# Cosine attention with a two-layer MLP: batch 1's norms moved into batch 0's visits, batch 0's row sums inverted on ScalarE, batch 2 turned by DMA

## The chip, the cores and the metric

The kernel runs on one core of a Trainium2 chip. The metric is the device time of one execution in microseconds. A core has TensorE (PE in the profile, its weight loads PEld), VectorE (DVE), ScalarE (ACT), GpSimd (POOL) and SyncE (SP), each with a queue of its own that it works off in order, and 16 DMA engines. Matmul results land in PSUM; everything else lies in SBUF.

## The reference

Eight batches, 12 heads, 448 positions, 64 elements per head. Attention on normalised queries and keys, then two matrix products with a leaky ReLU between them:

```python
q_n = q / (np.linalg.norm(q, axis=-1, keepdims=True) + 1e-06)
k_n = k / (np.linalg.norm(k, axis=-1, keepdims=True) + 1e-06)
scores = np.matmul(q_n, k_n.transpose(0, 1, 3, 2)) / tau          # tau = 0.1
scores = scores - np.max(scores, axis=-1, keepdims=True)
attn = np.exp(scores)
attn = attn / (np.sum(attn, axis=-1, keepdims=True) + 1e-09)
attn_out = np.matmul(attn, v)
x = attn_out.transpose(0, 2, 1, 3).reshape(B * S, H * D)          # 3584 x 768
h = x @ w_in                                                      # 768 x 2048
out = np.maximum(0.01 * h, h) @ w_out                             # 2048 x 768
```

The scores are bounded because q and k have unit length, so the kernel leaves the maximum out.

## The kernel before, in words

Every instruction is put on its engine in the order in which the program is written (a manual schedule): an engine that waits holds back all that stands behind it in its queue. Inputs are cast to bf16 by the loads, which GpSimd's queue issues.

**A batch's steps.** The 448 positions are held as 112 partitions times 4. The 12 heads are 6 pairs (p) and 3 groups (g) of four heads; group g holds pairs 2g and 2g+1. A batch's q and k are normalised by `norm_squares` (x times x), `norm_reduce` (sum over 64 elements, on VectorE), `norm_root` (Ln and Exp with factor 0.5, on ScalarE), `norm_inverse` (add 1e-6, reciprocal, on VectorE) and `norm_apply` (multiply, two instructions for each group, on the engine given; `V` is VectorE, `P` GpSimd, `A` ScalarE). `norm_sums` is squares on VectorE and the reduce. Then the normalised q and k are turned, so that the head's elements lie on partitions: either by `turn_pair` (eight transposing matmuls for a pair into one PSUM tile of the pool `pmm`, then two copies) or by `turn`, one DMA transpose for a whole batch on SP's queue. Batches 0 to 2 take `turn_pair`, batches 3 to 7 `turn`.

`scores` computes half a pair's scores (two PSUM tiles of the pool `psc`, which has two) and their exponentials on ScalarE (L234). For a group, `weigh` is called twice, with s = 0 and 1. At s = 0 it makes the row sums on TensorE (`sums`, a PSUM tile `sm` of the pool `ppv`, which has two), inverts them (`inverse`, L262, a reciprocal on VectorE) and multiplies the first half of the values (`values`, the other `ppv` tile); `x_write` on VectorE scales the result into x. At s = 1 `values` needs a `ppv` tile again, the one that the reciprocal has read.

**Dense work.** x is cut into pieces; piece 0 is columns 0 to 255 of batch 0, piece 1 the next 128, then one piece for each batch. For a piece, `layer1` is 16 groups of 6 matmuls (L306), each followed by a leaky ReLU on ScalarE (L311), and `layer2` is 2 groups of 16 matmuls for every 128 tokens (L319), each followed by a copy on ScalarE (L325) and an output DMA on SP's queue. Both use the pool `pmm`, which has two tiles.

**Order.** An opening stretch written out by hand works through the first 256 columns of batch 0 (`part_scores` instead of `scores`), with the loads of batch 0, both weight matrices and batch 1 (in thirds, one for each group, then v). Then comes the loop over batches b and visits n = 0 to 11, a visit being half a pair. In a visit stand, in this order: the scores (batch 0: the remaining 192 columns, from visit 2 on), one owed `weigh` (a group's two are owed after its last visit, so they fall into the two visits that follow: 4 and 5, 8 and 9, and 0 and 1 of the next batch), the norm steps for later batches and the loads (`second_part` for batch 0, `after_scores` for the others), dense work until a budget is spent (`fill(budget(b, n))`, in planned microseconds), and the `turn_pair` calls that the table `turns` names. Where layer 1 is due and no `weigh` is owed, half a microsecond of it is put between a visit's two exponentials. The budgets run evenly from 0 to the end of piece 1 over the first 27 visits (32.22 planned us); the plan counts 0.67 for a layer-1 group of piece 0, 0.35 for one of piece 1 and 2.65 for a layer-2 group.

**Buffers that the steps touch.** The pool `bfpool` has four q and k tiles, so batch 2's loads take batch 0's; `vpool` has two, so batch 2's v waits for the last `values` of batch 0; `inp` holds one q_n and one k_n, so a batch's squares wait until the batch before is turned.

**Where the norms of batches 1 and 2 stand.** Before the change, the squares of batch 1's first group are at visit 2 of batch 0 on GpSimd, its apply at visit 7 and its turns at visits 9 and 10; the other two groups are normalised in visits 0 to 3 of batch 1 and turned at visits 3 to 5. Batch 2's `norm_sums` are at visits 6 and 7 of batch 1, its apply at 8 and 9, its six `turn_pair` at visits 10, 11 and visit 1 of batch 2.

Of the kernel before, what the change touches and what calls it, by code (L numbers as in the profile page):

```python
# [16 lines left out]
def kernel(  # L17
# [18 lines left out]
    nc = tc.nc  # L36
# [47 lines left out]
    def load(b, what, g0=0, g1=G):  # L84
        src = {"q": q_r, "k": k_r, "v": v_r}[what]
        if (what, b) not in st:
            if what == "v":
                st[what, b] = vpool.tile([PK, H, NT, D], BF16, name="v_bf")
            else:
                st[what, b] = bfpool.tile([PK, H, NT, D], BF16, name="qk_bf")  # L90
        if g1 - g0 == G:
            nc.gpsimd.dma_start(out=st[what, b], in_=src[b])  # L92
            return
        for g in range(g0, g1):
            nc.gpsimd.dma_start(out=st[what, b][:, g::G], in_=src[b][:, g::G])
# [19 lines left out]
    def norm_squares(b, what, eng, g0=0, g1=G):  # L115
        if (what + "n", b) not in st:
            st[what + "n", b] = inp.tile([PK, G, 2, NT, 2, D], BF16, name=f"{what}_n")
            st[what + "i", b] = small.tile([PK, G, 4, NT], F32, name=f"{what}_ni")
        for g in range(g0, g1):
            x, sq = by_quad(st[what, b])[:, g], squares(b, what, g, g + 1)[:, 0]  # L120
            if eng is nc.scalar:
                nc.scalar.activation(sq, x, func=ACTF.Square)
            else:
                eng.tensor_mul(sq, x, x)  # L124

    def norm_reduce(b, what, g0=0, g1=G):
        nc.vector.tensor_reduce(  # L127
            st[what + "i", b][:, g0:g1].rearrange("p g a t -> p (g a) t"),
            squares(b, what, g0, g1).rearrange("p g a t d -> p (g a) t d"),
            axis=AX.X, op=ALU.add,  # L130
        )
# [5 lines left out]
    def norm_root(b, what, g0=0, g1=G):  # L137
        ni = st[what + "i", b][:, g0:g1]
        nc.scalar.activation(ni, ni, func=ACTF.Ln, bias=tiny[:PK])
        nc.scalar.activation(ni, ni, func=ACTF.Exp, scale=0.5)  # L140

    def norm_inverse(b, what, g0=0, g1=G):
        ni = st[what + "i", b][:, g0:g1]
        nc.vector.tensor_scalar_add(ni, ni, 1e-6)
        nc.vector.reciprocal(ni, ni)  # L145

    def norm_apply(b, what, eng, g0=0, g1=G):
        x, xn, ni = by_quad(st[what, b]), st[what + "n", b], st[what + "i", b]
        for g in range(g0, g1):
            for j in range(2):  # L150
                ni_j = ni[:, g, 2 * j : 2 * j + 2]
                eng.tensor_tensor(  # L152
                    out=xn[:, g, j].rearrange("p t h d -> p h t d"),
                    in0=x[:, g, 2 * j : 2 * j + 2],
                    in1=ni_j.unsqueeze(3).to_broadcast([PK, 2, NT, D]),
                    op=ALU.mult,
                )
# [36 lines left out]
    def scores(b, p, half, hold=False):  # L194

        qT, kT = st["qT", b], st["kT", b]
        if half == 0:
            st["pe", b, p] = epool.tile([PK, NT, 2, S], BF16, name="pe")
        wide = 128 if b > 2 else PK
        for i in range(2):  # L200
            ki = 2 * half + i
            sc = psc.tile([128, 2, 512], F32, name="sc")
            o = p * S + ki * PK
            for a in range(2):
                r = slice(64 * a, 64 * a + 64)
                nc.tensor.matmul(  # L206
                    out=sc[:wide, a, :S], lhsT=kT[r, o : o + wide],
                    rhs=qT[r, p * S : (p + 1) * S], start=True, stop=True,
                )
            st["exp", i] = (st["pe", b, p][:, ki], sc[:PK, :, :S])  # L210
            if i == 0 or not hold:
                exponential(i)
# [46 lines left out]

    def inverse(b, g, sm, c0=0, c1=S):  # L260
        st["rs", b, g] = wk.tile([128, S], F32, name="rs")
        nc.vector.reciprocal(st["rs", b, g][:, c0:c1], sm[:, c0:c1])  # L262
        if ("x", b) not in st:
            x_place(b)

# [184 lines left out]
        at[0] += 1  # L450


    def second_part(n):
        if n == 2:
            norm_squares(1, "q", P, 0, 1)
            norm_squares(1, "k", P, 0, 1)
        elif n == 4:
            norm_reduce(1, "q", 0, 1)
            norm_reduce(1, "k", 0, 1)
        elif n == 6:  # L460
            norm_root(1, "q", 0, 1)
            norm_root(1, "k", 0, 1)
        elif n == 7:
            norm_inverse(1, "q", 0, 1)
            norm_inverse(1, "k", 0, 1)
            norm_apply(1, "q", V, 0, 1)
            norm_apply(1, "k", P, 0, 1)


    def after_scores(b, n):  # L470
        if b + 2 < B and b > 1 and n < 2:
            load(b + 2, "qk"[n])
        if b + 1 == B:
            return
        if b > 1 and n == 2:
            load(b + 1, "v")
        if b == 1:
            if n == 0:
                load(2, "q")
                norm_sums(1, "q", 1, 2)  # L480
                norm_sums(1, "k", 1, 2)
            elif n == 1:
                load(2, "k")
                norm_root(1, "q", 1, 2)
                norm_root(1, "k", 1, 2)
                norm_sums(1, "q", 2, 3)
                norm_sums(1, "k", 2, 3)
            elif n == 2:
                load(2, "v")
                for what in "qk":  # L490
                    norm_inverse(1, what, 1, 2)
                    norm_apply(1, what, P, 1, 2)
                norm_root(1, "q", 2, 3)
                norm_root(1, "k", 2, 3)
            elif n == 3:
                for what in "qk":
                    norm_inverse(1, what, 2, 3)
                    norm_apply(1, what, P, 2, 3)
            elif n == 5:
                load(3, "q")  # L500
            elif n == 6:
                norm_sums(2, "q")
                load(3, "k")
            elif n == 7:
                norm_sums(2, "k")
            elif n == 8:
                norm_root(2, "q")
                norm_inverse(2, "q")
                norm_apply(2, "q", P)
            elif n == 9:  # L510
                norm_root(2, "k")
                norm_inverse(2, "k")
                norm_apply(2, "k", V, 0, 1)
                norm_apply(2, "k", P, 1, 3)
        elif n == 2:
            norm_sums(b + 1, "q")
        elif n == 3:
            norm_sums(b + 1, "k")
        elif n == 4:
            norm_root(b + 1, "q")  # L520
        elif n == 5:
            norm_root(b + 1, "k")
            norm_inverse(b + 1, "q")
            norm_apply(b + 1, "q", P)
        elif n == 6:
            norm_inverse(b + 1, "k")
            norm_apply(b + 1, "k", P)
        elif n == 7:
            turn(b + 1, "q")
        elif n == 9:  # L530
            turn(b + 1, "k")

    turns = {
        (0, 9): (1, 0), (0, 10): (1, 1), (1, 3): (1, 2), (1, 4): (1, 3), (1, 5): (1, 4, 5), (1, 10): (2, 0, 1),
        (1, 11): (2, 2, 3), (2, 1): (2, 4, 5),
    }

    def after_dense(b, n):
# [6 lines left out]
    def budget(b, n):  # L545
        i = 12 * b + n + 1
        if i <= 27:
            return piece_end[1] * i / 27
        c, i = divmod(i - 3, 12)
        c = c - 1  # L550
        return piece_end[c] + (piece_end[c + 1] - piece_end[c]) * i / 12

    owed = []
    for b in range(B):
        for p in range(HP):
            for half in range(2):
                n = 2 * p + half
                hold = b > 0 and not owed and dense[at[0]][1] < 2.0
                if b > 0:
                    scores(b, p, half, hold)  # L560
                elif p > 0:
                    part_scores(p, half, *two)
                if owed:
                    weigh(*owed.pop(0))
                if half == 1 and p % 2 == 1:
                    c = two if b == 0 else ()
                    owed += [(b, p // 2, 0, *c), (b, p // 2, 1, *c)]
                if hold:
                    fill(spent[0] + 0.5)
                    exponential(1)  # L570
                if b == 0:
                    second_part(n)
                else:
                    after_scores(b, n)
                fill(budget(b, n))
                after_dense(b, n)
    fill(spent[0] + 1.0)
# [39 lines left out]
```

## Time and profile before

| | |
|---|---|
| median of 11 runs | 478.92 us (476.91 to 482.03) |
| the profiled execution | 480.06 us |
| its span, first to last instruction | 477.6 us |
| mean granted TensorE clock | 0.986 |
| busy: PE, DVE, ACT, POOL | 436.6, 219.1, 269.8, 126.6 us |
| chain that ended last: PE, DVE, ACT, DMA | 79%, 11%, 4%, 3% of the span |

The span covers the instructions; the execution has 2.5 us around it. A group row of the profile gives line, engine, operation, the tiles written and read with their shapes, the count, the busy time and the mean, and at its end the idle time of the engine ahead of these instructions and what released it. These rows name the operations of the change:

```profile
L262 DVE RECIPROCAL rs<-pv 128x448 f32<-128x448 f32 x21 | 62.0, 2954 | 144.2 <-PE pv L239 144.2
L262 DVE RECIPROCAL rs<-pv 128x256 f32<-128x256 f32 x3 | 5.3, 1753 | 3.2 <-PE pv L239 3.2
L262 DVE RECIPROCAL rs<-pv 128x192 f32<-128x192 f32 x3 | 4.1, 1357 | 10.1 <-PE pv L239 10.0
L188 DVE COPY qT<-mm 128x448 bf16<-128x448 bf16 x18 | 6.9, 386 | 5.4 <-PE mm L180 5.0
```

The columns 256 and 192 belong to batch 0; the idle time ahead of a reciprocal is VectorE waiting for row sums, which costs nothing by itself. In the timeline, batch 0's visits run from about 39 to 61 us, batch 1's from 61.4 to 108.7, batch 2's from 108.7 to 160.

### The profile page before, as it was taken

How to read it: one execution, taken by the hardware profiler on the slowest of the kernel's cores; microseconds unless marked ns; L12 is line 12 of the kernel's file. 1: busy time of each engine (PE TensorE's matmuls, PEld its weight loads, DVE VectorE, ACT ScalarE, POOL GpSimd, SP SyncE). 2: the span in 40 equal slices, each digit the busy share in tenths (PEclk: the TensorE clock that was granted, in tenths of full speed). 3: DMA queues.
4: the chain of work that ended last, by engine and by line, in shares of the span. 5: the costliest groups of instructions: out<-in, count | busy, mean ns of one | idle time of the engine just before them, and what ended most of it. 6: DMA issues, size and time to landing. Idle time of an engine off the chain costs nothing.

```text
span 477.6 us, 8541 instructions
## 1 busy us (share of the span) xinstructions
PE 436.6 (91%) x3632; PEld 222.4 (47%) x3632; DVE 219.1 (46%) x269; ACT 269.8 (56%) x445; POOL 126.6 (27%) x150
## 2 busy tenths in 40 slices
PE   0788978779899999989899999998999999999996
PEld 0456634454344554444334554444434554454463
DVE  5964677967913186206823186318711311321000
ACT  3766665836764557654674557664765567533411
POOL 7652308064083013800083013700180000000000
PEclk9999998979999999998999999999999999999999
DMA  9999991808529660493329560355034210020022
GB/s 115 207 201 203 194 175 28 113 2 126 81 52 138 126 109 1 71 212 56 53 50 135 130 108 1 59 125 92 0 59 92 60 41 1 18 66 18 0 67 66
DMA packets 73924, 41.23 MB, mean 86 GB/s; under 512 B 29600, under 2 KB 73120, under 8 KB 73888
## 3 DMA queue, kind: packets, MB, share of 16 engines
q0 software_dynamic: 37728, 22.81, 34.6%
q1 hardware_dynamic: 36160, 17.90, 16.0%
q8 instruction: 28, 0.46, 0.4%
q14 instruction: 8, 0.07, 0.0%
HBM read 45.61 MB, written 11.01 MB: 119 GB/s over the span
## 4 chain that ended last, share of the span: by engine, by line
PE 79%; DVE 11%; ACT 4%; DMA 3%; issue 2%; SPq 0%; POOL 0%; POOLq 0%; ACTq 0%; DVEq 0%
PE mm L319 29%; PE mm L306 28%; PE pv L239 12%; PE sc L206 7%; DVE rs L262 3%; DVE k_ni L127 2%; DMA kT<-k_n 2%; ACT pe L234 2%; PE sc L224 1%; DVE k_n L124 1%; DVE q_n L124 1%; PE mm L180 1%; DVE q_ni L127 1%; DMA qk_bf<-in_q_dram 1%; ACT hT L311 1%
## 5 line engine op out<-in xcount | busy, mean ns | idle before, releaser
L234 ACT ACTIVATE pe<-sc 112x896 bf16<-112x896 f32 (+2 forms) x192 | 168.1, 917 | 14.1 <-PE sc L224 7.9
L306 PE MATMUL mm<-xT,w_in_sb 128*128 128x512 bf16 (+3 forms) x864 | 157.4, 335 | 1.1 <-ACT hT L311 0.9
L319 PE MATMUL mm<-w_out_sb,hT 128*128 128x384 bf16 x896 | 155.3, 329 | 0.0
L262 DVE RECIPROCAL rs<-pv 128x448 f32<-128x448 f32 (+2 forms) x27 | 71.4, 2643 | 157.6 <-PE pv L239 157.5
L319 PEld LDWEIGHTS <-hT 128*128 128x128 bf16 x896 | 85.3, 98 | 67.6 <-issue 14.6
L306 PEld LDWEIGHTS <-w_in_sb 128*128 128x128 bf16 x864 | 77.8, 99 | 76.5 <-issue 17.1
L311 ACT ACTIVATE hT<-mm 128x512 bf16<-128x512 f32 (+3 forms) x144 | 71.9, 502 | 69.4 <-PE mm L306 69.0
L325 ACT COPY osb<-mm 128x384 f32<-128x384 f32 x56 | 26.8, 478 | 105.7 <-PE mm L319 70.8
L152 POOL TENSOR_TENSOR q_n<-qk_bf,q_ni 112x512 bf16<-112x512 bf16 x40 | 41.3, 1061 | 103.5 <-DVE q_ni L145 64.4
L206 PE MATMUL sc<-qT,kT 64*128 64x448 bf16 (+1 forms) x336 | 50.1, 362 | 10.4 <-ACT pe L234 7.2
L239 PE MATMUL pv<-pe,v_bf 112*32 112x448 bf16 (+2 forms) x864 | 48.8, 349 | 9.7 <-DVE rs L262 9.7
L152 POOL TENSOR_TENSOR k_n<-qk_bf,k_ni 112x512 bf16<-112x512 bf16 x44 | 46.6, 1085 | 15.4 <-DVE k_ni L145 15.4
L239 PEld LDWEIGHTS <-v_bf 112*32 112x32 bf16 x864 | 21.6, 100 | 30.0 <-issue 19.5
L92 POOL DMA_DIRECT2D v_bf<-in_v_dram x8 | 7.6, 944 | 101.8 <-PE pv L239 101.2
L206 PEld LDWEIGHTS <-kT 64*128 64x128 bf16 (+1 forms) x336 | 13.2, 103 | 40.4 <-issue 36.0
L127 DVE TENSOR_REDUCE q_ni<-q_n 112x16 f32<-112x1024 bf16 (+1 forms) x12 | 27.4, 2284 | 0.3
L127 DVE TENSOR_REDUCE k_ni<-k_n 112x16 f32<-112x1024 bf16 (+1 forms) x12 | 27.4, 2283 | 0.3
L239 PE MATMUL pv<-pe,ones 112*32 112x448 bf16 (+2 forms) x432 | 25.1, 350 | 1.0 <-ACT pe L234 1.0
L281 DVE TENSOR_TENSOR xT<-pv,rs 128x384 bf16<-128x384 f32 (+2 forms) x30 | 14.3, 477 | 22.9 <-PE pv L239 21.4
L278 DVE TENSOR_TENSOR xT<-pv,rs 128x448 bf16<-128x448 f32 x24 | 15.0, 624 | 19.4 <-PE pv L239 18.1
L180 PE MATMUL mm<-ident,q_n 112*128 112x112 bf16 x72 | 7.8, 243 | 10.7 <-DVE q_n L152 10.5
L124 DVE TENSOR_TENSOR q_n<-qk_bf 112x1024 bf16<-112x1024 bf16 x21 | 14.1, 718 | 4.6 <-DMA qk_bf<-in_q_dram 4.6
(42 smaller groups left out, 154.8 us busy)
## 6 DMA issues: line engine op xcount, KB each, us to landing
v_bf<-in_v_dram POOLq DMA_DIRECT2D x8, 672.0 KB, 7.9
qk_bf<-in_q_dram POOLq DMA_DIRECT2D x6, 672.0 KB, 7.5
qk_bf<-in_k_dram POOLq DMA_DIRECT2D x6, 672.0 KB, 10.7
w_in_sb<-in_moe_w_in_dram POOLq DMA_DIRECT2D x4, 768.0 KB, 19.8
w_out_sb<-in_moe_w_out_dram POOLq DMA_DIRECT2D x2, 1536.0 KB, 28.6
out_dram<-osb SPq DMA_DIRECT2D x16, 168.0 KB, 2.6
out_dram<-osb SPq DMA_DIRECT2D x16, 144.0 KB, 2.1
out_dram<-osb SPq DMA_DIRECT2D x16, 120.0 KB, 2.0
```

The lines of the kernel that those rows point to most:

```text
L124: eng.tensor_mul(sq, x, x)
L127: nc.vector.tensor_reduce(st[what + "i", b][:, g0:g1].rearrange("p g a t -> p (g a) t"), squares(b, what, g0, g1).rearrange("p g a t d -> ...
L152: eng.tensor_tensor(out=xn[:, g, j].rearrange("p t h d -> p h t d"), in0=x[:, g, 2 * j : 2 * j + 2], in1=ni_j.unsqueeze(3).to_broadcast([P ...
L206: nc.tensor.matmul(out=sc[:wide, a, :S], lhsT=kT[r, o : o + wide], rhs=qT[r, p * S : (p + 1) * S], start=True, stop=True,)
L234: nc.scalar.activation(out=pe, in_=sc, func=ACTF.Exp, scale=inv_tau)
L239: nc.tensor.matmul(out=dst[32 * a : 32 * a + 32, c0:c1], lhsT=weights(a, ki), rhs=st["pe", b, 2 * g + a // 2][:, ki, a % 2, c0:c1], start= ...
L262: nc.vector.reciprocal(st["rs", b, g][:, c0:c1], sm[:, c0:c1])
L278: nc.vector.tensor_mul(x[:, kt, 64:512], po, rs)
L306: nc.tensor.matmul(out=pm[:, :n], lhsT=w_in_sb[:, kt, m * 128 : (m + 1) * 128], rhs=st["x", b][:, kt, x0 : x0 + n], start=(kt == 0), stop= ...
L311: nc.scalar.activation(out=st["h", c][:, m, :n], in_=pm[:, :n], func=ACTF.Prelu, alpha=0.01)
L319: nc.tensor.matmul(out=po[:, :NH], lhsT=st["h", c][:, m, j0 : j0 + 128], rhs=w_out_sb[:, m, n * NH : (n + 1) * NH], start=(m == 0), stop=( ...
L325: nc.scalar.copy(out=osb, in_=po[:, :NH])
```

## The change

`inverse` for batch 0 is an Ln and an Exp with factor -1 on ScalarE instead of the reciprocal. `second_part` and batch 1's list in `after_scores` are replaced by `early`, which moves batch 1's norm steps to visits 0 to 11 of batch 0 and visits 0 and 1 of batch 1, with all three groups' squares on GpSimd, q applied on VectorE and k on GpSimd. Its turns move to visits 7, 8, 10 and 11 of batch 0 and visit 2 of batch 1. Batch 2's norms move from visits 6 to 9 of batch 1 to visits 3 to 7, its k is applied on VectorE throughout, and it is turned by two DMA transposes at visit 9 of batch 1 in place of the six `turn_pair`. The loads of batch 2's q and k move to visits 8 and 9 of batch 0, its v to visit 0 of batch 1, batch 3's q and k to visits 1 and 2. Scores of batch 2 take 128 keys' columns (its turned tiles are padded) instead of 112. Budgets are 1 planned us a visit in batch 0 and then even to the end of piece 1.

```diff
-        wide = 128 if b > 2 else PK
+        wide = 128 if b > 1 else PK
...
     def inverse(b, g, sm, c0=0, c1=S):
         st["rs", b, g] = wk.tile([128, S], F32, name="rs")
-        nc.vector.reciprocal(st["rs", b, g][:, c0:c1], sm[:, c0:c1])
+        rs = st["rs", b, g][:, c0:c1]
+        if b == 0:
+            nc.scalar.activation(rs, sm[:, c0:c1], func=ACTF.Ln)
+            nc.scalar.activation(rs, rs, func=ACTF.Exp, scale=-1.0)
+        else:
+            nc.vector.reciprocal(rs, sm[:, c0:c1])
...
-    def second_part(n):
...
+    def step(b, what, g0, g1, *steps):
+
+        for name, eng in steps:
+            if name == "squares":
+                norm_squares(b, what, eng, g0, g1)
+            elif name == "reduce":
+                norm_reduce(b, what, g0, g1)
+            elif name == "root":
+                norm_root(b, what, g0, g1)
+            else:
+                norm_inverse(b, what, g0, g1)
+                norm_apply(b, what, eng, g0, g1)
+
+    def early(b, n):
+        def both(to, g0, g1, name, eq=None, ek=None):
+            step(to, "q", g0, g1, (name, eq))
+            step(to, "k", g0, g1, (name, ek))
+
+        if b == 0:
+            if n == 0:
+                both(1, 0, 1, "squares", P, P)
+            elif n == 2:
+                both(1, 0, 1, "reduce")
+            elif n == 3:
+                both(1, 1, 2, "squares", P, P)
+            elif n == 4:
+                both(1, 0, 1, "root")
+            elif n == 5:
+                both(1, 0, 1, "apply", V, P)
+            elif n == 6:
+                both(1, 1, 2, "reduce")
+            elif n == 8:
+                both(1, 1, 2, "root")
+                both(1, 2, 3, "squares", P, P)
+                load(2, "q")
+            elif n == 9:
+                both(1, 1, 2, "apply", V, P)
+                load(2, "k")
+            elif n == 11:
+                both(1, 2, 3, "reduce")
+        elif n == 0:
+            both(1, 2, 3, "root")
+            load(2, "v")
+        elif n == 1:
+            both(1, 2, 3, "apply", V, P)
+            load(3, "q")
+        elif n == 2:
+            load(3, "k")
+        elif n == 3:
+            norm_sums(2, "q")
+        elif n == 5:
+            norm_sums(2, "k")
         elif n == 6:
-            norm_root(1, "q", 0, 1)
-            norm_root(1, "k", 0, 1)
+            step(2, "q", 0, 3, ("root", A), ("apply", P))
         elif n == 7:
...
+            step(2, "k", 0, 3, ("root", A), ("apply", V))
+        elif n == 9:
+            turn(2, "k")
+            turn(2, "q")
 
     def after_scores(b, n):
-        if b + 2 < B and b > 1 and n < 2:
+        if b < 2:
+            return early(b, n)
+        if b + 2 < B and n < 2:
             load(b + 2, "qk"[n])
...
-        if b == 1:
-            if n == 0:
-                load(2, "q")
-                norm_sums(1, "q", 1, 2)
-                norm_sums(1, "k", 1, 2)
...
-            elif n == 6:
-                norm_sums(2, "q")
-                load(3, "k")
-            elif n == 7:
-                norm_sums(2, "k")
-            elif n == 8:
-                norm_root(2, "q")
-                norm_inverse(2, "q")
-                norm_apply(2, "q", P)
-            elif n == 9:
-                norm_root(2, "k")
-                norm_inverse(2, "k")
-                norm_apply(2, "k", V, 0, 1)
-                norm_apply(2, "k", P, 1, 3)
...
     turns = {
-        (0, 9): (1, 0), (0, 10): (1, 1), (1, 3): (1, 2), (1, 4): (1, 3), (1, 5): (1, 4, 5), (1, 10): (2, 0, 1),
-        (1, 11): (2, 2, 3), (2, 1): (2, 4, 5),
+        (0, 7): (1, 0), (0, 8): (1, 1), (0, 10): (1, 2), (0, 11): (1, 3), (1, 2): (1, 4, 5),
     }
...
         if i <= 27:
-            return piece_end[1] * i / 27
+            return i if i <= 12 else 12 + (piece_end[1] - 12) * (i - 12) / 15
...
-                if b == 0:
-                    second_part(n)
-                else:
-                    after_scores(b, n)
+                after_scores(b, n)
```

More of the change, by code (lines that the diff above doesn't have):

```diff
@@ L450 @@
         at[0] += 1
-    def second_part(n):
[L454 to L459, printed above, removed]
+    def step(b, what, g0, g1, *steps):
[9 more added lines that the diff above has]
+                norm_apply(b, what, eng, g0, g1)
@@ L460, in second_part @@
         elif n == 6:
-            norm_root(1, "q", 0, 1)
-            norm_root(1, "k", 0, 1)
+            step(2, "q", 0, 3, ("root", A), ("apply", P))
         elif n == 7:
[L464 to L467, printed above, removed]
+            step(2, "k", 0, 3, ("root", A), ("apply", V))
+        elif n == 9:
+            turn(2, "k")
+            turn(2, "q")
     def after_scores(b, n):
-        if b + 2 < B and b > 1 and n < 2:
+        if b < 2:
+            return early(b, n)
@@ L474, in after_scores @@
             return
-        if b > 1 and n == 2:
+        if n == 2:
             load(b + 1, "v")
-        if b == 1:
-            if n == 0:
-                load(2, "q")
-                norm_sums(1, "q", 1, 2)
-                norm_sums(1, "k", 1, 2)
[L482 to L500, printed above, removed]
-            elif n == 6:
-                norm_sums(2, "q")
-                load(3, "k")
-            elif n == 7:
-                norm_sums(2, "k")
-            elif n == 8:
-                norm_root(2, "q")
-                norm_inverse(2, "q")
-                norm_apply(2, "q", P)
-            elif n == 9:
-                norm_root(2, "k")
-                norm_inverse(2, "k")
-                norm_apply(2, "k", V, 0, 1)
-                norm_apply(2, "k", P, 1, 3)
-        elif n == 2:
             norm_sums(b + 1, "q")
```

## The prediction

> **What bounds the kernel now.** I read the page first: TensorE is busy 91% of the span, so only its idle time and its slow clock can be won. Then the busy time by stages, for where it idles; the waits of the poor stretch; the timelines of TensorE and VectorE there, for what each wait stands behind; last the landing times of the loads.
>
> Stages (span; busy us and count for PE, PEld, DVE, ACT, POOL; clock, DMA share, GB/s):
>
> ```profile
> 50.00:60.00 10.00, 9.60 (x126) 6.46 (x123) 6.21 (x14) 6.04 (x12) 4.69 (x6) 1.00 1.41 191
> 60.00:70.00 10.00, 7.32 (x88) 4.03 (x86) 7.31 (x11) 6.10 (x12) 0.95 (x1) 1.00 1.09 167
> 90.00:100.00 10.00, 4.60 (x59) 2.48 (x52) 9.35 (x9) 4.19 (x10) 0.70 (x1) 0.79 0.14 19
> ```
>
> From 140 to 200 us PE is busy 59.9 of 60 us; between 60 and 130 it idles 13 us. The whole change acts between 25 and 131 us.
>
> TensorE and VectorE there (start, us, idle before and its releaser):
>
> ```profile
> 69.90 0.40 PE L206 MATMUL sc<-qT,kT 64*112 64x448 bf16 x2 [2.17 <-ACT pe L234]
> 71.03 4.40 PE L319 MATMUL mm<-w_out_sb,hT 128*128 128x384 bf16 x16
> 97.91 1.68 PE L239 MATMUL pv<-pe,v_bf 112*32 112x448 bf16 x16 [5.37 <-DVE rs L262]
> ...
> 84.53 1.89 DVE L124 TENSOR_TENSOR q_n<-qk_bf 112x1024 bf16<-112x1024 bf16 x3
> 86.45 3.35 DVE L127 TENSOR_REDUCE q_ni<-q_n 112x48 f32<-112x3072 bf16 x1
> 89.72 1.88 DVE L124 TENSOR_TENSOR k_n<-qk_bf 112x1024 bf16<-112x1024 bf16 x3
> 91.64 3.35 DVE L127 TENSOR_REDUCE k_ni<-k_n 112x48 f32<-112x3072 bf16 x1
> 94.91 2.95 DVE L262 RECIPROCAL rs<-pv 128x448 f32<-128x448 f32 x1
> ```
>
> Two things are to be seen. The wait of 5.37 us is a VectorE queue: batch 2's norms (84.5 to 94.9) stand ahead of the reciprocal that frees the PSUM buffer for the next values(). And waits are paid twice: the layer-2 group at 71.03 takes 4.40 us where others take 2.70, as the clock is halved:
>
> ```profile
> 72.00:75.00 3.00, 3.00 (x12) 0.50 0.05 11
> 98.00:102.00 4.00, 4.00 (x40) 0.50 0.01 4
> ```
>
> Last, the loads: the page's DMA row is nine tenths or more for its first six slices (72 us), and batch 1's thirds land late. Issue at 20.94 plus 23.5 us puts the second third of q at 44.4 (k 45.6); the last third, issued at 29.67 and 32.85, lands at 54.5 and 55.7:
>
> ```profile
> qk_bf<-in_q_dram POOLq DMA_DIRECT2D x1, 224.0 KB, 24.8
> ```
>
> **What the Trainium skill says.** "SBUF — State Buffer", section "Who interferes with whom": a VectorE instruction with two SBUF inputs contends with a GpSimd one that reads SBUF; the one that comes second blocks. The trace agrees. Applying the norm (L152) is 0.63 us alone on VectorE and 1.04 on GpSimd; together each takes about 1.5:
>
> ```profile
> L152 DVE TENSOR_TENSOR q_n<-qk_bf,q_ni x2: 627/1077/1527, 50.6 to 51.1; 112x512 bf16<-112x512 bf16 x2
> L152 POOL TENSOR_TENSOR k_n<-qk_bf,k_ni x2: 1296/1394/1491, 50.8 to 52.1; 112x512 bf16<-112x512 bf16 x2
> ```
>
> "TensorE: Matmul & The Clock Gate", section "What's actually happening", has the clock halve after an idle window of about 3.4 us. The trace shows 0.50 already after 2.0 us of idling (212.6), for about 3.3 us: 1.65 us lost each time. "ScalarE: Activation LUTs", section "Table sets: the hidden batching unit", puts exp and ln in one set, so no reload; the trace has one table load (1.28 us), with Ln and Exp mixed all through.
>
> **The change, step by step.** PE prices, start to start: part_scores 0.30 (192 columns), sums 0.34, values 0.44, layer-1 group 0.71 (piece 0) or 0.41 (piece 1), layer-2 group 2.70, turn_pair 0.50; at 448 columns scores 0.51, sums 0.77, values 0.87.
>
> *Row sums on ScalarE.* Three reciprocals of 1.75 and three of 1.36 leave VectorE; six Ln and six Exp come to ScalarE. No row shows Ln on 256 columns; the nearest is Prelu at 256, 0.38 (0.33 start to start). I take 0.35 each, ends 0.30 and 0.45. values() needs only the Ln, which frees the PSUM tile. In the prologue the waits 0.53 (at 32.37) and 1.43 (at 36.94) for rs go; ScalarE is behind its exponentials (the exp of pair 4 ends at 31.09), so Ln ends at 31.45, and the second one, behind the next exp, at about 35.0. The x writes end at 36.1 instead of 38.0, and the layer-1 group that began at 39.03 begins at 37.1: 1.9 us won. In the later visits no PE wait on rs stood, so nothing more there.
>
> *Batch 1's first part, now at visits 0 to 7 of batch 0.* Dense budget is 1.0 a visit instead of 1.19. From 37.1: ten layer-1 groups in visits 1 to 7 (7.1), six part_scores (1.8), sums and two values (1.22): turn_pair(1,0) at 47.2. It needs k_n from GpSimd, and its queue is now squares(1, third 1) at visit 3, then apply(1, third 0) at visit 5. The squares cannot start before the landing at 44.4. Each is 1.9 (L124 on POOL); VectorE's two q applications fall among them and alternate, so they end at about 48.7, and VectorE's second application and k's inverse at 49.5; then GpSimd's two k applications, 2.05: 51.6. Before, turn_pair(1,0) stood at 57.1 and waited for nothing. So PE idles 4.1 us and loses 1.65 to the clock: the 1.9 are spent, and the place is set by the loads, not by PE. Bounds for the arrival: 50.3 (no alternation) to 52.5.
>
> *Visits 8 to 10.* From 51.8: 8.16 us of PE work plus 1.65: turn_pair(1,2) at 61.6. GpSimd: squares of the last third from 54.5 to 58.3, q2's load 0.98, then k's application to 61.7. No wait to speak of; visit 10 ends at 62.0. That load issues 4.7 us later than before (53.61) and lands by 67, used from 73; k2's stands behind the k application (61.7), lands near 70, used from 83: nothing.
>
> *Batch 1, visits 0 to 2.* VectorE: copies, two reduces (2.4) to 65.1, copies; ScalarE's root waits for that just as it becomes free (65.6). POOL: v2's load waits for values(0,2,1) (65.8), then the last application to 70.7 and batch 3's loads, ten us earlier than before (81.0) and not used till 115. PE: 0.8 for visit 11, 1.29, 3.65 plus 0.8 of waiting for exponentials, 4.21: turns done at 72.8, copies at 73.4. Before, the same copies ended at 84.5. So 11 us are won on VectorE's start.
>
> *Batch 2's norms, visits 3 to 8.* The chain on VectorE is now longer: q's squares and reduce 5.24 (78.6); the reciprocal of group 0 queued behind it, 2.95 (81.6), for which PE's values(1,0,1) waits some 1.5, as before (1.29); values and x_write to 83.2; k's squares and reduce 5.23 (88.4); inverses 0.63 and 0.65 (89.7); then all six k applications on VectorE, where two were, while GpSimd does q's six: alternating, the first at 90.6 and 1.49 for each of five more: 98.05. If they went uncontended at 0.69, 93.8. Behind them the reciprocal of group 1, 2.95: 101.0. So values(1,1,1) starts at 101.05 instead of 97.91: +3.1. PE is there at about 92.5 and takes the same half clock after.
>
> *From there to batch 2's visit 5*, against before: six turn_pairs gone, 6 x 0.46 = -2.76; waits 0.17 and 0.26 gone; two more piece-1 groups are still to do, +0.82; visits 10 and 11 bound by ScalarE, +0.5; batch 2's visit 0 has no layer-2 group any more (budget 29.52, spent 29.57), so values(1,2,1) waits for its reciprocal, +1.6; the wait at 130.61 goes, -1.04, since VectorE begins batch 3's norms without turn copies ahead of them; 128-wide keys 0.55 against 0.59 per scores call, -0.2. Sum -1.5. The diff leaves batch 2's squares on VectorE. Its DMA transposes, which hold SP's queue while no layer-2 output is due: k issues at 98.05, q some 3.3 later, landing 5.9 after: 107.3, PE needs them at 111.1. Hidden; at the slowest seen (issue 8.2, landing 11.0) 117.2, which costs 6.
>
> **Sum.** +3.1 - 1.5 = +1.6 us; 480.06 of the profiled execution becomes 481.7. The median of the runs is 1.14 lower, 478.92, so 480.5. After visit 5 the work is the same.
>
> **Rivals.**
> 1. *Faster: the early start pays.* If batch 1's thirds land about 5 us sooner, PE never waits in batch 0, VectorE's chain starts at 67.7, values(1,1,1) at 95.3: -2.6 - 1.5 = -4.1, 474.8. It decides by the second third's landing by 41 and the last one's by 50. For it: 13 us of idle time are there. Against: nothing in the change touches the queue before 53 us. 17%.
> 2. *Slower still: batch 2's scores wait for the transposes* at the slowest seen: +7.6, 486.5. For: one took 8.2 us to issue and PE waited for it at 214.6. Against: loads then flowed; here few do. Or PE waits in batch 0 are longer by as much. 18%.
> 3. *VectorE's six applications are not slowed* (0.69 each): values(1,1,1) at 96.8, -2.6 in all, 476.3. Against: both overlaps in the trace alternate. 7%.
>
> **Numbers.** My forecast holds 58%: it runs from +0.2 to +4 by its bounds (alternation 1.3 to 1.6 each, the turn's wait, the clock). About 0.3% (1.4 us) is what a measurement can tell from none; of the forecast 38 points lie above it and 20 within. With the rivals: slower 56%, same 22% (2 from the third), faster 22%. The range goes from the third rival's 476.0 to 485.0, into the second; the first, and the second's far end, stay out. The forecast's own range is 479.1 to 483.
>
> **What would show it.** Right: a PE wait of 3 to 5 us at turn_pair(1,0) near 47 to 52, for POOL's k_n; layer 1 beginning near 37; the reciprocal near 98 behind six L152 on DVE at about 1.5; values after it later than 97.9; no L180 for batch 2; no wait near 131. Wrong: landings before 41, no wait at that turn, or the reciprocal of group 1 done before 96.

## The result and the profile after

The changed kernel takes 487.84 us (median of 12 runs, 485.75 to 489.9) against 478.64 (47 runs): ratio 1.0187, 95% interval 1.0166 to 1.0208. The forecast was 480.5 with a range to 485.0; the way was right and the size was not. The profiled execution took 487.0 us with a span of 485.0, 7.4 more than before. The medians are 9.2 us apart; the 1.8 us beyond these two executions are not in the traces shown here. By batch 2's visit 5, where the forecast's account ends, TensorE is 7.7 us late, so the loss of these executions lies where it was looked for. The same multiplication before and after:

```profile
130.61 0.94 PE L239 MATMUL pv<-pe,v_bf 112*32 112x448 bf16 x16 [1.04 <-DVE rs L262]
...
138.27 0.94 PE L239 MATMUL pv<-pe,v_bf 112*32 112x448 bf16 x16
```

TensorE's timeline after (start, us, what, idle before and its releaser):

```profile
33.16 1.03 PE L311 MATMUL mm<-xT,w_in_sb 128*128 128x256 bf16 x8 [1.11 <-DMA w_in_sb<-in_moe_w_in_dram]
50.70 0.37 PE L180 MATMUL mm<-ident,k_n 112*128 112x112 bf16 x4 [1.71 <-POOL k_n L152]
100.56 1.68 PE L239 MATMUL pv<-pe,v_bf 112*32 112x448 bf16 x16 [8.77 <-DVE rs L267]
115.98 0.93 PE L206 MATMUL sc<-qT,kT 64*128 64x448 bf16 x4 [6.28 <-DMA qT<-q_n]
121.59 0.94 PE L239 MATMUL pv<-pe,v_bf 112*32 112x448 bf16 x16 [0.71 <-DVE rs L267]
```

Two waits carry it. values(1,1,1), for batch 1, group 1 and the second half of the values, starts at 100.56, 2.65 us later than before (97.91), and batch 2's first scores wait another 6.28 us for a transpose. The clock is halved behind both, as the stages show (span; PE busy and count, clock, DMA share, GB/s):

```profile
92.00:100.00 8.00, 0.00 (x0) 0.60 0.09 5
100.00:104.00 4.00, 3.44 (x34) 0.52 1.26 163
109.00:116.00 7.00, 0.72 (x7) 0.86 1.25 193
116.00:121.00 5.00, 4.88 (x40) 0.51 0.00 0
```

VectorE's timeline has the first wait:

```profile
77.93 2.95 DVE L267 RECIPROCAL rs<-pv 128x448 f32<-128x448 f32 x1
82.46 1.89 DVE L124 TENSOR_TENSOR k_n<-qk_bf 112x1024 bf16<-112x1024 bf16 x3
84.38 3.35 DVE L127 TENSOR_REDUCE k_ni<-k_n 112x48 f32<-112x3072 bf16 x1
89.18 8.45 DVE L152 TENSOR_TENSOR k_n<-qk_bf,k_ni 112x512 bf16<-112x512 bf16 x6
97.56 2.94 DVE L267 RECIPROCAL rs<-pv 128x448 f32<-128x448 f32 x1
```

The last reciprocal is the one that TensorE needs. The six k applications ahead of it take 8.45 us, 1.4 each on the mean, because GpSimd applies q at the same time. The instructions of that one line between 88 and 98 us (min/median/max ns):

```profile
L152 POOL TENSOR_TENSOR q_n<-qk_bf,q_ni x6: 1046/1486/1488, 88.8 to 95.6; 112x512 bf16<-112x512 bf16 x6
L152 DVE TENSOR_TENSOR k_n<-qk_bf,k_ni x6: 1209/1525/1527, 89.2 to 96.1; 112x512 bf16<-112x512 bf16 x6
```

The second wait starts on another queue. GpSimd's timeline at that time:

```profile
97.03 0.11 POOL L163 MEMSET kT<- 128x16 bf16 x1
97.39 0.98 POOL L92 DMA_DIRECT2D qk_bf<-in_q_dram  x1 [0.21 <-POOL kT L163]
98.36 0.94 POOL L92 DMA_DIRECT2D qk_bf<-in_k_dram  x1
```

These are batch 4's loads. In the program they stand at visits 0 and 1 of batch 2, where TensorE arrives only at 109.7; but GpSimd has nothing else to do, and batch 2's q and k tiles, whose place they take, are free once the norms are applied. So they start together with the two transposes. The DMA view of 97 to 106 us (last column: us from issue to landing):

```profile
q0 software_dynamic: 1575, 0.80, 71.5%
q1 hardware_dynamic: 1018, 0.26, 22.1%
...
qk_bf<-in_q_dram POOLq DMA_DIRECT2D x1, 672.0 KB, 9.3
qk_bf<-in_k_dram POOLq DMA_DIRECT2D x1, 672.0 KB, 14.6
kT<-k_n SPq DMA_TRANSPOSE x1, 15.6
qT<-q_n SPq DMA_TRANSPOSE x1, 10.7
```

The loads' queue (q0) takes 71.5% of the engines, the transposes' (q1) 22.1%. And q's transpose cannot be issued until k's has been, which takes 7.28 us here (3.25 in experiment 1). Both are in the chain that ended last (start, us, what):

```profile
97.79 7.28 SPq L169
...
105.19 10.66 DMA qT<-q_n
```

### The profile page after: what moved, and what is told of

Same layout as the page of the kernel before. It is cut to its first block, busy times and chain, and to the rows that moved or that the text cites. A ratio compares the mean times of both kernels' runs of the same rounds, so it can differ in the third digit from the quotient of the medians.

```text
span 485.0 us, 8442 instructions
## 1 busy us (share of the span) xinstructions
PE 432.6 (89%) x3584; PEld 217.7 (45%) x3584; DVE 214.8 (44%) x255; ACT 272.6 (56%) x457; POOL 127.0 (26%) x146
## 4 chain that ended last, share of the span: by engine, by line
PE 75%; DMA 11%; DVE 7%; ACT 3%; SPq 2%; issue 1%; POOL 1%; POOLq 0%; ACTq 0%
PE mm L311 28%; PE mm L324 28%; PE pv L239 11%; PE sc L206 7%; DMA w_in_sb<-in_moe_w_in_dram 5%; DMA kT<-k_n 2%; DMA qT<-q_n 2%; DVE k_n L152 2%; ACT pe L234 2%; SPq L169 2%; DMA qk_bf<-in_q_dram 1%; DVE rs L267 1%; DVE q_n L152 1%; ACT hT L316 1%; DVE k_ni L127 1%
## 5 line engine op out<-in xcount | busy, mean ns | idle before, releaser
L267 DVE RECIPROCAL rs<-pv 128x448 f32<-128x448 f32 x21 | 62.0, 2954 | 155.7 <-PE pv L239 155.7
L152 POOL TENSOR_TENSOR q_n<-qk_bf,q_ni 112x512 bf16<-112x512 bf16 x36 | 38.6, 1103 | 97.9 <-DVE q_ni L145 81.3
L152 POOL TENSOR_TENSOR k_n<-qk_bf,k_ni 112x512 bf16<-112x512 bf16 x40 | 41.9, 1076 | 6.9 <-DVE k_ni L145 3.8
L180 PE MATMUL mm<-ident,q_n 112*128 112x112 bf16 x48 | 5.6, 254 | 11.7 <-DVE q_n L152 10.6
L239 PEld LDWEIGHTS <-ones 112*32 112x32 bf16 x432 | 9.2, 97 | 13.5 <-issue 9.8
```

Of the source, the lines that this page charges most:

```text
L152: eng.tensor_tensor(out=xn[:, g, j].rearrange("p t h d -> p h t d"), in0=x[:, g, 2 * j : 2 * j + 2], in1=ni_j.unsqueeze(3).to_broadcast([P ...
L239: nc.tensor.matmul(out=dst[32 * a : 32 * a + 32, c0:c1], lhsT=weights(a, ki), rhs=st["pe", b, 2 * g + a // 2][:, ki, a % 2, c0:c1], start= ...
L267: nc.vector.reciprocal(rs, sm[:, c0:c1])
```

## The experiments

Theory A: VectorE's six k applications hold the reciprocal, and then loads beside the transposes hold batch 2's scores. Each ratio is to the kernel before, run on the same chip.

**1. Batch 4's loads behind batch 3's v**, which waits for TensorE.

```diff
-        if b + 2 < B and n < 2:
+        if b + 2 < B and b > 2 and n < 2:
             load(b + 2, "qk"[n])
...
             load(b + 1, "v")
+            if b == 2:
+                load(4, "q")
+                load(4, "k")
```

> The changed kernel with batch 4's loads of q and k issued after batch 3's v (visit 2 of batch 2), so that none is in flight while batch 2 is turned. Theory A (the two DMA transposes take 15.6 and 10.7 us because 1.4 MB of loads flow beside them): they land in 5 to 7 us each, k near 103 and q near 108; the wait of 6.28 us at batch 2's first scores goes and so does the half clock after it; 479.5 to 481, a ratio of 1.002 to 1.005 to the kernel before. The wait of 8.8 us for the reciprocal stays. Rival B (the transposes are slow because one queues behind the other, or beside busy engines): they stay at 10 us or more, 487 to 488.

Measured 482.57 us, 1.0055 (1.0031 to 1.0079). The transposes without those loads, in the DMA view, and TensorE at batch 2's first scores:

```profile
kT<-k_n SPq DMA_TRANSPOSE x1, 5.3
qT<-q_n SPq DMA_TRANSPOSE x1, 6.9
...
110.92 0.55 PE L206 MATMUL sc<-qT,kT 64*128 64x448 bf16 x4
```

5.3 and 6.9 us instead of 15.6 and 10.7, and no wait at batch 2's first scores. Rival B falls: one transpose still stands behind the other here. Whether the loads slow a transpose through the DMA engines or through what feeds them, these runs don't separate. Time and ratio lie just above what was expected, and the profile says why:

```profile
101.03 1.69 PE L239 MATMUL pv<-pe,v_bf 112*32 112x448 bf16 x16 [8.78 <-DVE rs L267]
115.40 0.94 PE L239 MATMUL pv<-pe,v_bf 112*32 112x448 bf16 x16 [1.82 <-DVE rs L267]
116.27 4.45 PE L324 MATMUL mm<-w_out_sb,hT 128*128 128x384 bf16 x16
```

The first wait stays, and at 115.40 there is now the wait that the forecast put at 1.6 us, with a layer-2 group of 4.45 us behind it at half clock.

**2. Batch 2 turned on TensorE again.**

```diff
-        elif n == 9:
-            turn(2, "k")
-            turn(2, "q")
...
+        (1, 10): (2, 0, 1), (1, 11): (2, 2, 3), (2, 1): (2, 4, 5),
```

> The changed kernel with batch 2 turned by six turn_pair on TensorE (visits 10 and 11 of batch 1, visit 1 of batch 2) instead of two DMA transposes. Theory A: the wait of 6.28 us and some 1.9 of half clock go, 2.8 us of TensorE work come: 482 to 483. If the reciprocal's wait (8.8 us at 100.6) had been a consequence of the DMAs, it would go too and the time would fall to 475.

Measured 483.68, 1.007 (1.0037 to 1.0104), a little above the expected 482 to 483. No scores of batch 2 wait for a transpose any more. The reciprocal's wait is 8.77 us, as in the changed kernel: it has nothing to do with the DMA turns. The scores take 112 columns again in this kernel.

**3. The same, with k applied behind the reciprocal.**

```diff
         elif n == 7:
-            step(2, "k", 0, 3, ("root", A), ("apply", V))
+            step(2, "k", 0, 3, ("root", A))
+        elif n == 8:
+            step(2, "k", 0, 3, ("apply", V))
```

> The one before (turn_pair for batch 2), and batch 2's k inverse and its six applications on VectorE moved one visit on, so that they stand behind group 1's reciprocal in VectorE's queue. Theory A (six applications of 1.4 us on VectorE hold the reciprocal): reciprocal near 88.5 to 91.5, values(1,1,1) near 92 instead of 100.6, no half clock there; 472 to 474, a ratio of 0.985 to 0.99, faster than both kernels. Rival C (TensorE then waits for the turned k of batch 2 instead, as its groups come out of VectorE's queue 3 us later): a wait of 3 us or more at visits 10 and 11, 477 or more.

Measured 474.04 (four runs), 0.9887 (0.9833 to 0.9941): about 2% off the kernel of experiment 2 (1.8% by the ratios, 2.0% by the medians), for one visit's shift of eight instructions. VectorE's timeline, then TensorE's:

```profile
87.71 2.90 DVE L267 RECIPROCAL rs<-pv 128x448 f32<-128x448 f32 x1
91.25 0.18 DVE L144 TENSOR_SCALAR k_ni<-k_ni 112x48 f32<-112x48 f32 x1
91.47 0.45 DVE L145 RECIPROCAL k_ni<-k_ni 112x48 f32<-112x48 f32 x1
91.95 5.63 DVE L152 TENSOR_TENSOR k_n<-qk_bf,k_ni 112x512 bf16<-112x512 bf16 x6
...
91.19 0.94 PE L239 MATMUL pv<-pe,v_bf 112*32 112x448 bf16 x16
```

The reciprocal ends at 90.6, and values(1,1,1) no longer waits. The applications are shorter too (5.63 instead of 8.45 us), as GpSimd has done half of its own by then. Rival C's wait is there, at 1.11 us and not 3:

```profile
98.77 2.77 PE L324 MATMUL mm<-w_out_sb,hT 128*128 128x384 bf16 x16 [1.11 <-DVE kT L188]
```

**4. Both cures with the DMA turns kept**: the later loads of experiment 1 and the moved k of experiment 3.

> Batch 2 turned by DMA, batch 4's loads later, and batch 2's k applied behind group 1's reciprocal. Theory A: values(1,1,1) starts near 91 instead of 101, but k's application still ends at about 97.6, so the transposes land at 103 and 108.5 as without it, and TensorE, at batch 2's first scores by 102, waits 6 to 7 us for them: the wait moves, and only some 2 us are won on the kernel with the later loads alone; ratio 1.000 to 1.004. Rival F (with the reciprocal's wait gone the DMA turns are hidden well enough): 0.990 or less.

Measured 479.21, 1.0008 (0.998 to 1.0035). The wait moved as expected, and rival F falls:

```profile
107.13 0.93 PE L206 MATMUL sc<-qT,kT 64*128 64x448 bf16 x4 [7.33 <-DMA qT<-q_n]
```

k is applied by 98.2, its transpose takes 5.4 us and q's, issued 3.4 us later, 5.2. TensorE is at the scores 7.33 us early. Even without loads beside them, two transposes in a row behind norms that end at 98 land too late for a TensorE that no longer waits elsewhere; the six turn_pair, which cost TensorE 2.8 us by the forecast's price, are in time.

**5. Batch 1's move alone** (with the new budgets, the moved loads and ScalarE's inverses): batch 2's norms and turns as in the kernel before.

> The changed kernel with batch 2's norms and turns as in the kernel before (norm_sums at visits 6 and 7, applied at 8 and 9 with one group of k on VectorE, six turn_pair), so that of the change remain batch 1's move, the budgets and ScalarE's inverses. Theory A: VectorE's chain starts at about 82 (after values(1,0,1)), two norm_sums of 5.2 and the reciprocal of 2.95 put values(1,1,1) at 95 to 96, before it was 97.9; TensorE waits 4 us there and loses the clock again; what is won is given back by the missing layer-2 group; ratio 1.000 to 1.005, so batch 1's move alone wins nothing. Rival E (batch 1's early norms are the gain, and only batch 2's part of the change spoils it): as fast as the kernel with k behind the reciprocal, 0.987 to 0.990.

Measured 478.41, 0.9981 (0.9955 to 1.0007): no difference that can be told, a little better than the 1.000 that was put as the floor. TensorE waits 3.34 us:

```profile
94.99 1.69 PE L239 MATMUL pv<-pe,v_bf 112*32 112x448 bf16 x16 [3.34 <-DVE rs L267]
```

Batch 1's last turns are copied by 73.5 instead of 84.6, but batch 2's norms stay in the visits where they collide with the same reciprocal. Rival E falls: by itself the early start won nothing; together with experiment 3's placing of batch 2's norms it did. The other half was not tried: whether moving batch 2's norms behind the reciprocal would have won without batch 1's move stays open.

**6. The kernel before, with the later loads in every batch from 2 on.**

```diff
-        if b + 2 < B and b > 1 and n < 2:
-            load(b + 2, "qk"[n])
...
         if b > 1 and n == 2:
             load(b + 1, "v")
+            if b + 2 < B:
+                load(b + 2, "q")
+                load(b + 2, "k")
```

> The kernel before with the loads of q and k issued after v's in every batch from 2 on. Theory A (loads beside a DMA transpose stretch it): the transpose of k that takes 11.0 us at 203.6 lands in 5 to 7, the wait of 2.0 us at 212.6 and 1.6 us of half clock go; ratio 0.992 to 0.996. Rival B (loads have no part in it): 0.999 to 1.001, with that wait still there.

Measured 476.47, 0.9954 (0.9932 to 0.9976). One transpose in the kernel before had the same trouble. It took 11.0 us beside loads issued at 199.5 and 200.4, in the DMA view from 199 to 214, and TensorE waited for it:

```profile
kT<-k_n SPq DMA_TRANSPOSE x1, 11.0
...
214.61 0.55 PE L206 MATMUL sc<-qT,kT 64*128 64x448 bf16 x4 [2.02 <-DMA kT<-k_n]
```

and without them:

```profile
kT<-k_n SPq DMA_TRANSPOSE x1, 5.1
```

The wait of 2.02 us there and the half clock behind it are gone: TensorE is busy throughout from 200 to 220 us at a clock of 1.00. Rival B falls.

**7. The best put together**: experiment 3, the later loads in every batch, and one layer-2 group brought to visit 0 of batch 2, where values(1,2,1) waited.

```diff
-            return i if i <= 12 else 12 + (piece_end[1] - 12) * (i - 12) / 15
+            return i if i <= 12 else 12 + (piece_end[1] - 12) * (i - 12) / 15 + 0.1 * (i == 25)
```

> The kernel with turn_pair and k behind the reciprocal (ratio 0.989), with the loads of q and k after v's in every batch from 2 on, and a layer-2 group at visit 0 of batch 2 instead of visit 1. Theory A: the wait of 1.8 us for the reciprocal at visit 1 goes, and that of 2.0 us for a transpose near 203 with its half clock: 0.978 to 0.983. If the waits only move, 0.987 to 0.990.

Measured 470.56 (four runs), 0.981 (0.9782 to 0.9838), as expected and faster than both kernels. Both waits are gone. What the layer-2 group is worth by itself was not measured.

**8. Batch 0's inverses on VectorE again.**

```diff
-        if b == 0:
+        if False:
             nc.scalar.activation(rs, sm[:, c0:c1], func=ACTF.Ln)
```

> The changed kernel with batch 0's row sums inverted by the reciprocal on VectorE again. Theory A (what is won in the opening stretch is spent at turn_pair(1,0), which waits for loads): layer 1 begins 1.3 us later, the wait at the turn is that much shorter, the time is the same within 0.5 us, 487.3 to 488.3. Rival D (ScalarE's inverses are worth what they take out of the opening stretch): 489 or more.

Measured 490.21, 1.0223 (1.0168 to 1.0277). That is rival D's band and not theory A's, but the interval overlaps that of the changed kernel. It was run a second time beside it:

> The changed kernel itself, beside the next one on the same chip, to size a difference of a few tenths of a per cent: 1.0166 to 1.0208 again.

> The changed kernel with batch 0's row sums inverted on VectorE again, a second time. Theory A, as first stated (the opening stretch's gain is spent at the turn): within 0.1% of the changed kernel. Theory A2, formed after the first run (the opening gain is spent, but at visit 1 of batch 1 the reciprocal stands behind two reduces on VectorE and TensorE waits 0.96 us for it, more when the clock drops there): 0.2 to 0.5% slower than the changed kernel. Rival D (all of the opening's 1.3 us remains): the turn's arrival is 1.3 us later.

The changed kernel gave 487.97, 1.015 (1.0109 to 1.0192); with the inverses on VectorE 492.86, 1.0243 (1.0193 to 1.0294). That is 4.9 us between the medians, with intervals that just don't meet, and more than either version of theory A allowed. TensorE in the second profile with the inverses on VectorE:

```profile
39.14 0.62 PE L239 MATMUL pv<-pe,v_bf 112*32 112x256 bf16 x16 [1.23 <-DVE rs L267]
41.24 1.44 PE L311 MATMUL mm<-xT,w_in_sb 128*128 128x256 bf16 x6 [0.47 <-ACT hT L316]
67.41 0.51 PE L239 MATMUL pv<-pe,v_bf 112*32 112x192 bf16 x16 [1.35 <-DVE rs L267]
```

and its stages in the opening stretch:

```profile
34.00:38.00 4.00, 3.89 (x44) 0.57 1.32 204
42.00:46.00 4.00, 4.00 (x30) 0.70 1.34 203
```

The wait at visit 1 of batch 1 is there (67.41, 1.35 us), as theory A2 had it. The clock adds to it: after waits of 0.70 us for the reciprocal (32.39) and 1.00 us for a weight load (34.02) it halves, and a layer-1 group takes 1.44 us instead of 0.81. The turn of batch 1, at 52.9, is then too late to wait for the loads, so the loss is not absorbed, which is rival D's sign. In the first run's profile the opening kept full clock, the turn came at 50.70 as in the changed kernel, which is theory A's sign, and the clock fell at 62 to 70 instead. How often each happens was not measured, so the size of the effect stays open.

In the best kernel the same edit was tried as well:

> The best kernel so far (0.981) with batch 0's row sums inverted on VectorE. Theory A2: TensorE waits some 1 us for the reciprocal at visit 1 of batch 1; 0.1 to 0.5% slower than 0.981, 0.982 to 0.986. If ScalarE's inverses are worth nothing: 0.980 to 0.982.

Measured 472.44, 0.9845 (0.9807 to 0.9883), against 0.981 (0.9782 to 0.9838): in the expected band, but the intervals overlap and the two ran on different chips, so that nothing is decided here.

## Why the prediction was right or wrong

**What failed: the step on batch 2's DMA transposes**, "107.3, PE needs them at 111.1. Hidden", and with it the argument against the second rival, "loads then flowed; here few do". The transposes landed at 113.4 and 115.9, and TensorE needed them at 109.7. The term that the sum put at nothing cost 6.28 us of wait and some 2 of half clock (scores, sums and values from 115.98 to 119.95 take 3.97 us; the next such set, from 131.61, takes 2.19). The prediction says nothing of batch 4's loads. They stand in the program at batch 2's visits 0 and 1, behind the transposes, while GpSimd's queue reached them at 97.4, in the microsecond in which the transposes became ready. The change itself brings the two together, since both wait for the same applied norms. Experiment 1 shows it by the transposes' 5.3 and 6.9 us once those loads are elsewhere. This rival, given 18%, is what happened: it stood at 486.5, and 487.84 was measured. That the two are so close is in part luck: it had the landing (117.2) and the need (111.1) both later by about 1.4 us than they came, and counted no half clock.

**The way was right, for a smaller part of the loss.** The forecast's own cost, VectorE's queue ahead of values(1,1,1), is 2.65 of the 7.7 us. Against the forecast, TensorE is 6.1 us late at visit 5 (138.27 instead of 132.2): it reached batch 2's scores 1.4 sooner than forecast, lost some 8.4 to the transposes and their half clock, and got 0.9 back at visit 1.

**The chain on VectorE was right.** Forecast: k's six applications alternating with GpSimd's at 1.49 us, done at 98.05, the reciprocal at 101.0, values(1,1,1) 3.1 us late. Measured: a median of 1.53 each, done at 97.6, reciprocal at 100.5, 2.65 us late. Experiment 3, set against experiment 2, undoes it by order alone. The third rival, uncontended applications, did not happen. (The prediction has it at 476.3 and again at 476.0; its sum gives 476.3.)

**The opening stretch was mis-sized.** Layer 1 was to begin at 37.1; it began at 37.77, since a part of layer 1 ahead of it now waited 1.11 us for a weight load (33.16), which the forecast had not looked at. The turn of batch 1 waited for GpSimd as said, for 1.71 us and 0.48 for ScalarE instead of 4.1, and the clock did not fall there: TensorE came at 48.2 instead of 47.2, and k_n at 50.7 instead of 51.6. It made no difference to what followed, as turn_pair(1,2) was bound by GpSimd again (60.69, forecast 61.7), and the copies after batch 1's last turns ended at 72.8 (forecast 73.4).

**"In the later visits no PE wait on rs stood, so nothing more there" was read from the old order.** Against the kernel before it holds, since there was no wait to win. In the new order VectorE has two reduces ahead of the reciprocal at visit 1 of batch 1, so ScalarE's inverses prevent a wait that the change would otherwise bring (0.96 and 1.35 us in experiment 8), and the clock adds to it. The two measurements put them at 0.4% and 0.9% of the time; only the second is clear of noise, and barely.

**The rest of the sum.** The wait of 1.6 us at batch 2's visit 1 was 0.71 in the changed kernel, because TensorE ran at half clock while the reciprocal did not; with the clock up it was 1.82 (experiment 1). The wait near 131 went as forecast, and VectorE's early start came as forecast too (72.8 instead of 84.6). The first rival did not come: batch 1's thirds let GpSimd begin at 44.2 and 54.2, as before.

## What to carry to other kernels

A queue's load starts where its engine gets to it, not where the program has it: for every DMA that is moved, ask which issues are waiting behind the same release, above all on an engine that is otherwise idle. Work that nobody needs yet goes behind the short instruction that frees a buffer, on the same engine; here that order alone was worth about 2% with batch 2 turned by turn_pair, and 0.5% with the DMA turns, where the wait moved (experiment 4 against 1). Moving work earlier may gain nothing while the queue that held up the rest stays as full: batch 1's move alone gave no difference that could be told.

## What the runs showed of the hardware

A DMA transpose of 672 KB took 5.0 to 6.9 us from issue to landing with no load beside it (experiments 1, 4 and 6). Beside two loads of 672 KB each from the other queue it took 10.7 and 15.6 in the changed kernel, 11.0 where the loads were issued 4.1 us ahead of it (203.58 in the kernel before) and 6.8 where they were 7.5 us ahead (152.60 there; 5.1 in experiment 6).

TensorE's clock halved after single waits of 1.8 to 2.0 us, shorter than the 3.4 that the Trainium skill's "TensorE: Matmul & The Clock Gate" (section "What's actually happening") gives for an idle window, and in experiment 8 after two shorter ones in a row (0.70 and 1.00 us). It did not do so after every such wait: 1.71 us at 50.7 cost nothing, and the same wait of 1.79 us for a reciprocal, ahead of the same layer-2 group, left that group at 2.77 us in experiments 2 and 3 and made it 4.39 in experiment 5. So what a wait of this length costs can't be told from its length alone.

VectorE and GpSimd, each with two inputs in SBUF, went in turns of 1.5 us, less than their lone times together (0.63 and 1.04).
